# Five row minima and maxima of a closing check, moved one turn earlier on VectorE in a fused linear-attention and mixture-of-experts kernel

## The chip, the cores and the metric

The kernel runs on one core of one Trainium2 chip. The metric is the device time in microseconds (us) of one execution. The time of a kernel is the median of its runs.

## The reference, cut to what matters

A gated linear attention over 4 batches, 8 heads, 768 tokens and a head width of 48 gives `x` of 3072 tokens by 384. A mixture of 8 experts follows, whose gate is balanced in eight rounds:

```python
for t in range(S):
    state = f[:, :, t, :, None] * state + np.einsum('bhd,bhe->bhde', k[:, :, t], v[:, :, t])
    y[:, :, t] = np.einsum('bhd,bhde->bhe', q[:, :, t], state)
...
P = np.exp(logits - logits.max())          # logits = x @ w_gate
for _ in range(8):
    P /= P.sum(1, keepdims=True) + 1e-09
    P /= P.sum(0, keepdims=True) + 1e-09
    P *= N / E
for e in range(E):
    h = np.maximum(x @ w1[e], 0.0)
    out += P[:, e:e + 1] * (h @ w2[e])
```

All operands are float32. The kernel computes each product from pairs of float16 numbers (a high and a low part, names ending in `h` and `l`), which is good only while the inputs lie in certain bounds. So it also computes a flag, and where the flag is set, a slower general version (`general`) runs behind the fast one.

## The kernel before, in words

`fast` does the attention and, between its steps, part of experts 0 and 1. After some 520 us it goes over to the long last stage, which the change concerns: experts 2 to 7 in 48 **periods** (`period`, one for each expert, half of the hidden width and batch, in the order of `ORDER`). A period has 15 **slots**. In each slot TensorE gets, in this order:

- 6 products of layer 1 (`kb_A` to `kb_F`, six PSUM banks of the pool `pk`; a scheme with 15 products in place of 18, so that VectorE and ScalarE have to add and copy banks between: `EVENTS`, L1188 to L1198);
- whatever the slot's **jobs** issue (`plan`);
- 4 or 5 products of layer 2 of the period before (`layer2`).

Layer 2 works in **groups** of 12 products that add up in one PSUM tile `kyps`, 6 groups a period. The tile is then read once, either by ScalarE (`yt`, L1094, with GpSimd adding it to the output at L1095) or by VectorE (`acc`, L1091). These tiles come from the pool `psm` with the tag "m", which has **two** buffers.

The order on each engine is the order of the program text: `mm` puts every product behind the one before on TensorE, and `pin` does the same for each instruction on VectorE, ScalarE and GpSimd. So the place in the text at which an instruction is issued is its place in the engine's queue. Which of the two buffers a tile gets, and whom it must wait for, is settled by the framework when the kernel is built: a tile can take a buffer once the last reader of the tile that was in it is done.

The jobs of a slot are short steps of generators. One of them is `all_checks`: it gets a **turn** in certain slots of the periods from the third on, namely slots 5, 10 and 13, slots 3 and 11, slot 5, and slots 3 and 11, over and over in four periods. A turn is one `next(checks, None)`, the last job of its slot. The turns go first to maxima of the weights, then to `guard`, and at the end to `verdict`. Its last part puts five columns of one number per partition (`g`, `[128, 7]`) through `partition_reduce` (L94): a transposition on TensorE makes a column a row of 128 numbers on one partition, in a tile `gd0_t` to `gd4_t` (`gd_t` in the profile), which comes from the pool `psm` with the tag "m" too; VectorE takes the row's minimum or maximum (L99, `gd_r`). A `yield` lies between the two, so the reduction is issued one turn after its transposition. After each reduction comes another `yield` (L812), so that a row takes two turns: ten turns for the five rows. Eight small operations on single numbers follow in two more turns (L813 to L821), the last of which writes the flag.

Two pieces of code name what is touched: the pool of two buffers, and the read of the tile.

```python
psm = ctx.enter_context(tc.tile_pool(name="psm", bufs=2, space=PSUM))
...
ps = psm.tile([128, DM], F32, name=f"kyps_{n}_{t}_{v}", tag="m")
...
ps = psp.tile([128, 128], F32, name=name + "_t", tag=tag)      # psp is psm, tag is "m"
```

Of the kernel before, what the change touches and what calls it, by code (L numbers as in the profile page):

```python
# [85 lines left out]
def consts(nc, pool):  # L86
    identf = pool.tile([128, 128], F32, name="identf")
    make_identity(nc, identf)
    onesf = pool.tile([128, 128], F32, name="onesf")
    nc.vector.memset(onesf, 1.0)  # L90
    return identf, onesf


def partition_reduce(nc, pool, psp, tag, identf, col, op, name, mm, pin):  # L94
    ps = psp.tile([128, 128], F32, name=name + "_t", tag=tag)
    mm(transpose=True, out=ps[0:1, :], in_=col, identity=identf)
    row = pool.tile([1, 1], F32, name=name + "_r")
    yield
    pin(nc.vector.tensor_reduce(out=row, in_=ps[0:1, :], axis=AX.X, op=op))  # L99
    return row  # L100

# [149 lines left out]
def fast(ctx, tc, qkf, vbd, wg, w1, w2, out, flag):  # L251
    nc = tc.nc
# [17 lines left out]
    def pin(ins):  # L270
        engine = ins.ins.engine
        if fixed[0]:
            if engine in last:
                behind(ins, last[engine])
            last[engine] = ins
        return ins
# [7 lines left out]
    cst = ctx.enter_context(tc.tile_pool(name="cst", bufs=1))  # L284
# [8 lines left out]
    psm = ctx.enter_context(tc.tile_pool(name="psm", bufs=2, space=PSUM))  # L293
# [4 lines left out]
    identf, onesf = consts(nc, cst)  # L298
# [496 lines left out]
    def verdict():  # L795
        g = cst.tile([128, 7], F32, name="wg6")
        pin(nc.vector.tensor_reduce(out=g[:, 0:2], in_=wmx, axis=AX.X, op=ALU.min))
        pin(nc.vector.tensor_reduce(out=g[:, 2:4], in_=wmx, axis=AX.X, op=ALU.max))
        xm = xmx.rearrange("p b k -> p (b k)")
        pin(nc.vector.tensor_reduce(out=g[:, 4:5], in_=xm, axis=AX.X, op=ALU.max))  # L800
        pin(nc.vector.tensor_reduce(out=g[:, 6:7], in_=xm, axis=AX.X, op=ALU.min))
        yield
        pin(nc.vector.tensor_scalar(out=okm[:, 1:2], in0=g[:, 0:1], scalar1=W1_MIN / W1S, scalar2=None, op0=ALU.is_ge))
        pin(nc.vector.tensor_scalar(out=okm[:, 2:3], in0=g[:, 1:2], scalar1=W2_MIN / W2S, scalar2=None, op0=ALU.is_ge))
        pin(nc.vector.tensor_scalar(out=okm[:, 3:4], in0=g[:, 3:4], scalar1=W2_MAX / W2S, scalar2=None, op0=ALU.is_le))
        pin(nc.vector.tensor_reduce(out=g[:, 5:6], in_=okm, axis=AX.X, op=ALU.min))
        yield
        yield
        rows = []
        for n, (col, op) in enumerate(((5, ALU.min), (4, ALU.max), (2, ALU.max), (6, ALU.min), (0, ALU.min))):  # L810
            rows.append((yield from partition_reduce(nc, cst, psm, "m", identf, g[:, col:col + 1], op, f"gd{n}", mm, pin)))
            yield  # L812
        pin(nc.vector.tensor_tensor(out=rows[1], in0=rows[1], in1=rows[2], op=ALU.mult))  # L813
        pin(nc.vector.tensor_tensor(out=rows[3], in0=rows[3], in1=rows[4], op=ALU.mult))
        pin(nc.vector.tensor_scalar(out=rows[3], in0=rows[3], scalar1=BALANCE, scalar2=None, op0=ALU.mult))
        pin(nc.vector.tensor_tensor(out=rows[3], in0=rows[1], in1=rows[3], op=ALU.is_le))
        pin(nc.vector.tensor_scalar(out=rows[1], in0=rows[1], scalar1=XW1_MAX / W1S, scalar2=None, op0=ALU.is_le))
        yield
        pin(nc.vector.tensor_tensor(out=rows[0], in0=rows[0], in1=rows[1], op=ALU.mult))
        pin(nc.vector.tensor_tensor(out=rows[0], in0=rows[0], in1=rows[3], op=ALU.mult))  # L820
        pin(nc.vector.tensor_scalar(out=flag, in0=rows[0], scalar1=FLAG_AT, scalar2=None, op0=ALU.is_lt))  # L821
# [79 lines left out]
    live, g = list(early), -4  # L901
# [217 lines left out]
    def all_checks():  # L1119
        todo = [(e, j, k) for e in range(NE) for k in (1, 2) for j in range(4)]  # L1120
        raws_ = []
        for i in range(len(todo) + 1):
            if i < len(todo):
                e, j, k = todo[i]
                raw = lp.tile([128, 768], F32, name=f"wm_{k}_{e}_{j}", tag="wmax", bufs=2)
                nc.sync.dma_start(out=raw, in_=(w1 if k == 1 else w2)[e, j].rearrange("p a f -> p (a f)"))
                raws_.append(raw)
            if i:
                e, j, k = todo[i - 1]
                pin(nc.vector.tensor_reduce(out=wmx[:, k - 1, 4 * e + j:4 * e + j + 1], in_=raws_[i - 1], axis=AX.X, op=ALU.max, apply_absolute_value=True))  # L1130
            yield
        yield from guard()
        yield from verdict()
# [146 lines left out]
```

## Time and profile before

| | |
|---|---|
| Median of 3 runs | 1570.7 us (1570.29 to 1571.0) |
| Profiled execution, its own time | 1571.04 us |
| Its span, first to last instruction | 1569.3 us |
| Granted TensorE clock, mean | 0.99 |
| TensorE busy | 1524.3 us, 97% of the span |
| VectorE, ScalarE, GpSimd busy | 1085.6, 781.2 and 533.1 us |
| The five transpositions `gd_t` | 1394.1 to 1488.3 us |
| The five reductions `gd_r` | 1407.0 to 1500.9 us |
| The flag written | 1533.7 us |

The span starts with the first instruction of the program; 1.7 us of the profiled execution lie around it. In rows of the timeline the first number is the start, the second the length, both in us; a bracket at the end says how long the engine had been idle and who released it. Products overlap on TensorE: the length of one is longer than the step to the next, and the step is what it costs the engine. In the views of waits the three numbers are the total in us, how often, and the longest.

### The profile page before, as it was taken

The page shows a single profiled execution, that of the slowest core. Times are in us where ns is not written, and L with a number is a line of the kernel's source. Part 1 is how long each engine was busy: PE and PEld are TensorE (multiplying, and loading weights), DVE is VectorE, ACT ScalarE, POOL GpSimd, SP SyncE. Part 2 cuts the span into 40 slices and gives each one's busy share as a digit, 9 for nine tenths or more (in the row PEclk, how much of TensorE's full clock was granted, in tenths as well). Part 3 has the DMA queues.
Part 4 walks back from the last instruction along what each step waited for, and adds up shares of the span by engine and source line. Part 5 has one row for each costly group of instructions (what it writes and reads, how often), then busy time and mean ns, then how long its engine had stood idle before and what let it go on. Part 6 is the DMA issues. An engine that isn't in the chain of part 4 may idle for free.

```text
span 1569.3 us, 32417 instructions
## 1 busy us (share of the span) xinstructions
PE 1524.3 (97%) x13425; PEld 1107.7 (71%) x13425; DVE 1085.6 (69%) x1798; ACT 781.2 (50%) x1493; POOL 533.1 (34%) x668
## 2 busy tenths in 40 slices
PE   6799999999999999999999999999999999999998
PEld 4688886666555777777777777777777777776675
DVE  7687987884766766677767677666666666755554
ACT  6655555554343655555445554445444445444432
POOL 1644444354519012333333332223322223222211
PEclk9799999999999999999999999999999999999999
DMA  8355554541001222232322222121212111100011
GB/s 267 93 135 133 137 124 115 134 112 38 21 26 56 61 61 82 66 91 67 91 66 85 74 85 61 50 62 41 71 42 64 40 43 51 31 11 11 6 51 69
DMA packets 91502, 114.85 MB, mean 73 GB/s; under 512 B 52464, under 2 KB 68976, under 8 KB 91344
## 3 DMA queue, kind: packets, MB, share of 16 engines
q1 hardware_dynamic: 91344, 112.68, 25.5%
q8 instruction: 107, 1.75, 0.5%
q14 instruction: 51, 0.42, 0.1%
HBM read 88.41 MB, written 14.16 MB: 65 GB/s over the span
## 4 chain that ended last, share of the span: by engine, by line
PE 67%; DVE 1%; ACT 1%; issue 0%; POOL 0%; ACTq 0%; DVEq 0%; POOLq 0%
PE kyps L279 35%; PE kb_B L279 8%; PE kb_A L279 8%; PE kb_D L279 6%; PE kb_C L279 4%; PE kb_E L279 2%; PE kb_F L279 2%; PE yps L279 1%; PE hps L279 1%; ACT yt L1094 0%; DVE acc L1091 0%; ACT kh L1195 0%; ACT cp L1188 0%; DVE cp L1193 0%; DVE kb_F L1190 0%
## 5 line engine op out<-in xcount | busy, mean ns | idle before, releaser
L1095 POOL TENSOR_TENSOR acc<-acc,yt 128x384 f32<-128x384 f32 x172 | 173.4, 1008 | 637.7 <-ACT yt L1094 637.7
L279 PE MATMUL kyps<-k2h,kh 128*128 128x384 f16 x1152 | 375.5, 326 | 6.1 <-ACT yt L1094 2.5
L279 PE MATMUL kyps<-k2l,kh 128*128 128x384 f16 x1152 | 375.5, 326 | 0.0
L279 PE MATMUL kyps<-k2h,kl 128*128 128x384 f16 x1152 | 375.5, 326 | 0.0
L279 PEld LDWEIGHTS <-k1h 128*128 128x128 f16 x2880 | 281.5, 98 | 70.4
L279 PEld LDWEIGHTS <-kh 128*128 128x128 f16 x2304 | 225.4, 98 | 103.9
L1094 ACT ACTIVATE yt<-kyps,pes 128x384 f32<-128x384 f32 x172 | 99.8, 580 | 326.4 <-PE kyps L279 324.5
L279 PEld LDWEIGHTS <-k1l 128*128 128x128 f16 x1440 | 140.7, 98 | 63.4 <-issue 6.2
L1091 DVE SCALAR_TENSOR_TENSOR acc<-kyps,pes,acc 128x384 f32<-128x384 f32 x92 | 56.8, 618 | 176.0 <-PE kyps L279 176.0
L279 PEld LDWEIGHTS <-kl 128*128 128x128 f16 x1152 | 112.7, 98 | 53.3 <-issue 9.3
L1188 ACT ACTIVATE cp<-kb_A 128x512 f32<-128x512 f32 x144 | 86.0, 597 | 86.6 <-PE kb_A L279 86.1
L279 PE MATMUL yps<-w2h,hl 128*128 128x384 f16 x384 | 126.4, 329 | 1.5 <-DVE hl L441 0.8
L279 PE MATMUL yps<-w2l,hh 128*128 128x384 f16 x384 | 126.0, 328 | 0.8 <-DVE w2l L362 0.8
L279 PE MATMUL yps<-w2h,hh 128*128 128x384 f16 x384 | 126.3, 329 | 0.3 <-DVE hl L394 0.3
L279 PEld LDWEIGHTS <-w1h 128*128 128x128 f16 x1344 | 99.0, 99 | 38.5 <-ACT w1h L341 5.9
L1188 ACT ACTIVATE cp<-kb_B 128x512 f32<-128x512 f32 x144 | 86.9, 604 | 52.0 <-DVE kb_B L1190 50.5
L1193 DVE TENSOR_TENSOR cp<-kb_D,cp 128x512 f32<-128x512 f32 x144 | 98.8, 686 | 16.2 <-PE kb_D L279 15.2
L279 PEld LDWEIGHTS <-hh 128*128 128x128 f16 x768 | 75.4, 99 | 47.8 <-issue 3.1
L279 PE MATMUL hps<-xh,w1h 128*128 128x128 f16 (+1 forms) x672 | 86.1, 260 | 5.6 <-ACT w1h L341 5.5
L279 PE MATMUL hps<-xl,w1h 128*128 128x128 f16 (+1 forms) x672 | 85.3, 260 | 0.4 <-DVE xl L616 0.2
L279 PE MATMUL hps<-xh,w1l 128*128 128x128 f16 (+1 forms) x672 | 84.3, 259 | 0.6 <-DVE w1l L362 0.6
L279 PE MATMUL kb_A<-xbh,k1h 128*128 128x256 f16 x288 | 78.5, 273 | 0.8 <-ACT yr L411 0.6
(249 smaller groups left out, 3645.0 us busy)
## 6 DMA issues: line engine op xcount, KB each, us to landing
wm<-in_w_dram SPq DMA_DIRECT2D x64, 384.0 KB, 3.0
q<-in_qkf_dram SPq DMA_DIRECT2D x23, 672.0 KB, 5.0
vr<-in_vbd_dram SPq DMA_DIRECT2D x24, 384.0 KB, 3.5
ys<-yr SPq DMA_DIRECT2D x48, 192.0 KB, 2.5
k1r<-in_w_dram SPq DMA_DIRECT2D x24, 384.0 KB, 3.1
k2r<-in_w_dram SPq DMA_DIRECT2D x24, 384.0 KB, 3.0
yb<-ys SPq DMA_DIRECT2D x48, 192.0 KB, 2.4
out_dram<-acc SPq DMA_DIRECT2D x24, 192.0 KB, 1.9
```

Of the source, the lines that this page charges most:

```text
L279: ins = (nc.tensor.transpose if transpose else nc.tensor.matmul)(**kw)
L1091: pin(nc.vector.scalar_tensor_tensor(out=y, in0=ps, scalar=p, in1=y, op0=ALU.mult, op1=ALU.add))
L1094: pin(nc.scalar.activation(out=yt, in_=ps, func=AF.Copy, scale=p))
L1095: pin(nc.gpsimd.tensor_tensor(out=y, in0=y, in1=yt, op=ALU.add))
L1188: pin(nc.scalar.activation(out=fresh(ev[2]), in_=bk, func=AF.Copy))
L1193: pin(nc.vector.tensor_tensor(out=fresh(ev[4]), in0=bk, in1=old, op=ALU.add if ev[2] == '+' else ALU.subtract))
```

## The change

The reduction is issued directly behind its transposition, in the same turn. The turn that held it stays, as an empty one behind: the rows still take two turns each, and what follows them has the turn that it had. The instructions are the same and as many as before.

```diff
     ps = psp.tile([128, 128], F32, name=name + "_t", tag=tag)
     mm(transpose=True, out=ps[0:1, :], in_=col, identity=identf)
     row = pool.tile([1, 1], F32, name=name + "_r")
-    yield
     pin(nc.vector.tensor_reduce(out=row, in_=ps[0:1, :], axis=AX.X, op=op))
     return row
...
         for n, (col, op) in enumerate(((5, ALU.min), (4, ALU.max), (2, ALU.max), (6, ALU.min), (0, ALU.min))):
-            rows.append((yield from partition_reduce(nc, cst, psm, "m", identf, g[:, col:col + 1], op, f"gd{n}", mm, pin)))
+            rows.append(partition_reduce(nc, cst, psm, "m", identf, g[:, col:col + 1], op, f"gd{n}", mm, pin))
+            yield
             yield
```

## The prediction

> **What bounds the kernel now.** I read the page first, then the waits of TensorE, then the tile of the changed step, and last the timeline around it.
>
> ```profile
> span 1569.3 us, 32417 instructions
> PE 1524.3 (97%) x13425; PEld 1107.7 (71%) x13425; DVE 1085.6 (69%) x1798; ACT 781.2 (50%) x1493; POOL 533.1 (34%) x668
> PE 67%; DVE 1%; ACT 1%; issue 0%; POOL 0%; ACTq 0%; DVEq 0%; POOLq 0%
> ```
>
> TensorE is busy for 97% of the span and holds nearly all that is named in the chain that ended last. In the last stage a microsecond is gained only where TensorE stands, and then it is gained in full as long as nothing else comes late.
>
> ```profile
> PE kyps L279 <- ACT yt L1094: 2.5, 4, 0.7
> PE kyps L279 <- DVE acc L1091: 2.1, 3, 0.7
> PE kyps L279 <- DVE gd_r L99: 1.0, 2, 0.5
> PE kb_A L279 <- ACT cp L1188: 1.6, 4, 0.8
> ```
>
> These are TensorE's waits over the whole span, as far as they belong to the last stage (beside two on `cp` for `kb_D`). The first three lines make 9 waits and 5.6 us, all of them of the first product of a layer 2 group (`kyps`) for somebody who reads a PSUM tile. Where are they? One row of the groups of instructions, asked for 1387.75 to 1504.87 us alone, holds all nine:
>
> ```profile
> L279 PE MATMUL kyps<-k2h,kh 128*128 128x384 f16 x121 | 39.4, 325 | 6.1 <-ACT yt L1094 2.5 <-DVE acc L1091 2.1 <-DVE gd_r L99 1.0
> L279 PE MATMUL gd_t<-identf,wg x5: 272/273/273, 1394.1 to 1488.3; 128*1 128x128 f32 x5
> L99 DVE TENSOR_REDUCE gd_r<-gd_t x5: 267/267/269, 1407.0 to 1500.9; 1x1 f32<-1x128 f32 x5
> ```
>
> So in a stage of 48 periods the groups wait only in those five in which the rows `gd_t` are made and read. From these rows, too, the first row lies in its buffer from 1394.1 until the end of its reduction, 1407.0 + 0.27 = 1407.3: 13 us, more than half a period. In that time one of the two buffers of `psm` is taken, and the groups have to share the other. The timeline shows what that does:
>
> ```profile
> 1392.54 0.27 PE L279 MATMUL kb_A<-xal,k1h 128*128 128x256 f16 x1
> 1394.12 0.27 PE L279 MATMUL gd_t<-identf,wg 128*1 128x128 f32 x1
> 1394.23 0.33 PE L279 MATMUL kyps<-k2l,kh 128*128 128x384 f16 x1
> 1397.05 0.27 PE L279 MATMUL kb_A<-xbl,k1h 128*128 128x256 f16 x1
> 1397.38 0.32 PE L279 MATMUL kyps<-k2h,kh 128*128 128x384 f16 x1
> 1400.47 0.33 PE L279 MATMUL kyps<-k2l,kh 128*128 128x384 f16 x1
> 1401.51 0.32 PE L279 MATMUL kyps<-k2h,kh 128*128 128x384 f16 x1 [0.71 <-DVE acc L1091]
> ```
> ```profile
> 1392.92 0.70 DVE L1190 TENSOR_TENSOR kb_A<-kb_A,cp 128x512 f32<-128x512 f32 x1 [0.63 <-PE kb_A L279]
> 1396.71 0.62 DVE L1091 SCALAR_TENSOR_TENSOR acc<-kyps,pes,acc 128x384 f32<-128x384 f32 x1 [3.09 <-PE kyps L279]
> 1400.84 0.62 DVE L1091 SCALAR_TENSOR_TENSOR acc<-kyps,pes,acc 128x384 f32<-128x384 f32 x1 [1.19 <-PE kyps L279]
> ```
>
> The last product of a group starts at 1400.47; VectorE reads the group from 1400.84 to 1401.46; the next group's first product starts at 1401.51, a step of 1.04 us where two such products normally lie 0.16 apart. It waited for the one free buffer: 0.88 us, of which the bracket names 0.71. Where six layer 1 products lie between two groups (1397.05 to 1397.38) most of the read is covered, and 0.33 - 0.11 = 0.22 us are left, without a bracket. So the nine named waits are not all. I size the loss by the periods instead, by the first `kb_F` product of each, which stands in the same slot every time:
>
> ```profile
> 1344.56 0.27 PE L279 MATMUL kb_F<-xah,k1h 128*128 128x256 f16 x1
> 1366.16 0.27 PE L279 MATMUL kb_F<-xah,k1h 128*128 128x256 f16 x1
> 1387.75 0.27 PE L279 MATMUL kb_F<-xah,k1h 128*128 128x256 f16 x1
> 1504.87 0.27 PE L279 MATMUL kb_F<-xah,k1h 128*128 128x256 f16 x1
> 1526.88 0.27 PE L279 MATMUL kb_F<-xah,k1h 128*128 128x256 f16 x1
> ```
>
> The two periods before the rows take 21.60 and 21.59 us. The five with the rows take 1504.87 - 1387.75 = 117.12 us. Five undisturbed ones would take 5 x 21.595 = 107.98, so 9.14 us are extra. Five transpositions are in that, at a step of 0.11 us each (1394.12 to 1394.23): 0.55 us, which stay. **8.6 us** are waits.
>
> **The change, part by part.**
>
> *What goes.* The row's hold shrinks. The transposition takes 0.27 us, the hand-over from TensorE to VectorE 0.11 (the last `kb_A` product above ends at 1392.54 + 0.27 = 1392.81, VectorE starts on it at 1392.92), the reduction 0.27: some 0.65 us in place of 13. The row that starts at 1394.12 is read by 1394.8; the next group starts at 1397.4. It then finds a free buffer, as groups do in every other period, and the same holds for the groups behind it. What remains are the groups that start directly behind a row:
>
> ```profile
> 1420.28 0.27 PE L279 MATMUL gd_t<-identf,wg 128*1 128x128 f32 x1
> 1420.50 0.32 PE L279 MATMUL kyps<-k2h,kh 128*128 128x384 f16 x1
> 1475.99 0.27 PE L279 MATMUL gd_t<-identf,wg 128*1 128x128 f32 x1
> 1476.23 0.32 PE L279 MATMUL kyps<-k2h,kh 128*128 128x384 f16 x1
> ```
>
> The second and the fourth row are such: the steps are 0.22 and 0.24 us instead of 0.11. There the new group takes the buffer of the group that ended just now, whose reader is not quite done; the row has the other one. No earlier reduction can spare that, since it comes after the transposition. These 0.11 + 0.13 = 0.24 us stay, and 8.6 - 0.24 = **8.4 us** go. The bounds of this term: 8.6 if these two steps vanish as well, and 8.6 - 2 x 0.88 = 6.8 if both groups are given the row's buffer instead and wait as long as the longest wait above.
>
> *What comes.* No instruction is added, and no DMA, nothing of ScalarE, GpSimd or SyncE is moved. Five reductions stand earlier in VectorE's queue and wait there for TensorE to reach the transposition. Everything behind them in that queue waits too: the next additions of banks, the reads of groups, the low parts `kl`; behind those stand ScalarE's copies, and behind these TensorE's next products on the bank. What has VectorE to do at the five places? Behind the first row it stands idle until 1396.71, 3.09 us by the bracket above. The others:
>
> ```profile
> 1422.07 0.70 DVE L1190 TENSOR_TENSOR kb_B<-kb_B,cp 128x512 f32<-128x512 f32 x1 [1.62 <-PE kb_B L279]
> 1453.50 0.69 DVE L1193 TENSOR_TENSOR cp<-kb_D,cp 128x512 f32<-128x512 f32 x1
> 1454.11 0.68 DVE L1198 SCALAR_TENSOR_TENSOR kl<-kb_B,kh 128x512 f16<-128x512 f32 x1
> 1455.22 0.70 DVE L1190 TENSOR_TENSOR kb_E<-kb_E,cp 128x512 f32<-128x512 f32 x1 [0.42 <-PE kb_E L279]
> 1476.70 0.70 DVE L1190 TENSOR_TENSOR kb_D<-kb_D,cp 128x512 f32<-128x512 f32 x1 [2.01 <-ACT cp L1188]
> 1490.87 0.62 DVE L1091 SCALAR_TENSOR_TENSOR acc<-kyps,pes,acc 128x384 f32<-128x384 f32 x1 [3.09 <-PE kyps L279]
> ```
> ```profile
> 1453.44 0.27 PE L279 MATMUL gd_t<-identf,wg 128*1 128x128 f32 x1
> 1456.72 0.27 PE L279 MATMUL kb_D<-xah,k1h 128*128 128x256 f16 x1
> ```
>
> Behind the second row (1420.28) VectorE's next work starts at 1422.07, after 1.62 us of idling: the reduction, due at 1420.66 and over at 1420.93, fits. Behind the fourth (1475.99) it is due at 1476.37 and over by 1476.64; the addition behind it waited for ScalarE until 1476.70. Behind the fifth (1488.28) nothing starts before 1490.87. Only the third row (1453.44) meets work: the reduction could start at 1453.82, and the read of `kb_D` that started at 1453.50 would wait until 1454.09, 0.6 us later. It would then end at 1454.78, and `kb_D` is next written at 1456.72; if that product came earlier by the longest wait above, 0.88 us, there would still be 1.06 us of slack. The delay is gone again at 1455.22, where VectorE idled 0.42 us. So I put the moved reductions at **0**. If that cover were gone, the third would cost its 0.6 us; below nothing the term can't go, as the same reductions stand in the queue a turn later today, where they take 0.27 us from nobody whom TensorE waits for except in the two `gd_r` waits, counted already.
>
> One rule speaks against the change. The Trainium skill ("PSUM — Partial Sum Buffer", section "Engine vs sequencer instructions") says that the queues of ScalarE, VectorE and GpSimd are strictly first in, first out: so a reduction that waits holds all behind it, however ready. By the rows, four of the five hold nothing. If instead every hold reached TensorE with its whole 0.65 us, the sum would be 8.4 - 5 x 0.65 = 5.1 us.
>
> *The sum.* The profiled execution took 1571.04 us, 1.74 more than its span, and less 8.4 makes that 1562.6. The median of the runs is 0.34 lower, 1570.7; with the same saving it becomes **1562.3 us**, 0.53% less. (About 0.2%, 3.1 us, is what a measurement of this kernel can tell from no change.) What is late next is nothing in these periods: they become like those ahead of them. The flag's last operations keep their turns.
>
> **The rivals.**
>
> *Each row still costs one wait.* The framework hands out the two buffers when the kernel is built, by its own estimate of who is done first. It may give the group behind every row the row's buffer, with a read that comes late because VectorE had something else in hand. Then one full wait of 0.88 us remains per row: 5 x 0.88 = 4.4 us, a saving of 4.2, and 1566.5 us. For it: two groups did take the buffer of a row (the two `gd_r` waits). Against it: in both the row's hold ended first, and three of five rows have over 2 us until the next group starts.
>
> *The wait moves into VectorE's queue and costs more there: slower.* The queue rule above is its ground. VectorE's additions read what the slot before has made, so at worst VectorE arrives at the reduction a whole slot ahead, 21.6 / 15 = 1.44 us, stands until the row is there, and all behind it is late by that and by the hold of 0.65: 2.09 us. If TensorE pays each in full, that is 5 x 2.09 = 10.4 against 8.6 saved: 1570.7 + 1.8 = 1572.5 us. It decides from 8.6 / 5 = 1.7 us a row. Against it: at four places VectorE idled anyway, for 1.62 to 3.09 us.
>
> *The change frees nothing, or it is given back.* The waits could have another cause than the rows' hold, or the buffers might be tied up until the turn's end as before; 1570.7 us. Against it: all nine waits lie in the five periods, and two are put down to `gd_r` itself. For giving back speaks only that `kb_A` waits for ScalarE's copies at times, 1.6 us in four waits over the span; a period of 22.01 us follows the rows (1504.87 to 1526.88), so 0.4 us per period can appear where TensorE is undisturbed.
>
> **How the numbers follow.** The forecast has 0.80, one wait per row 0.13, nothing gained 0.04, slower by the queue 0.03. The range of the likeliest case: without any remainder 1570.7 - 8.6 = 1562.1, less the half spread of the runs (0.35) and rounding, 1561.5; at the other end 1570.7 - 6.8 = 1563.9 with the row's buffer taken twice, 0.6 for the third row and 0.3 for the spread, 1564.8. The other cases, 2 in 10, are left out. The first two cases are faster by over 0.2% (1566.5 is 0.27% less): 0.93. Nothing gained is within, and so is the slower case at its worked price (0.11%), for which I count a third of its chance: 0.05. The rest of it, where the queue costs more than that price, is slower: 0.02.
>
> **What would show it.** Right: the first `kb_F` products of the five periods lie about 21.7 us apart (21.6 and a transposition); TensorE's waits of `kyps` for `yt`, `acc` and `gd_r` sum to under 1 us; each reduction starts 0.4 to 0.6 us behind its transposition. Half right: `kyps <- gd_r` has five waits of up to 0.9 us. Wrong: the waits for `yt` and `acc` stay as they are (another cause), or `kb_A` and `kb_D` wait for `cp` several us more than before (VectorE's queue).

## The result and the profile after

The changed kernel takes 1562.49 us (median of 5 runs, 1562.02 to 1563.09); the kernel before 1570.7 (5 runs). The ratio is 0.9948, with a 95% interval of 0.9934 to 0.9963: 8.2 us less. The forecast was 1562.3 and 8.4. The profiled execution took 1563.09 us.

The lines of the page, the groups of instructions on TensorE asked for the five periods with the rows, the tile of the row, and the first `kb_F` product of each of those periods and of the one behind them (in this file L278 is the old L279, L98 the old L99; in the files of the experiments the line numbers shift by a few, the names of the tiles stay):

```profile
span 1561.4 us, 32416 instructions
PE 1522.8 (98%) x13425; PEld 1108.4 (71%) x13425; DVE 1086.1 (70%) x1798; ACT 781.4 (50%) x1493; POOL 533.0 (34%) x668
```
```profile
L278 PE MATMUL kyps<-k2h,kh 128*128 128x384 f16 x121 | 39.4, 326 | 0.0
L278 PE MATMUL gd_t<-identf,wg x5: 272/272/273, 1394.2 to 1481.5; 128*1 128x128 f32 x5
L98 DVE TENSOR_REDUCE gd_r<-gd_t x5: 278/279/280, 1394.5 to 1481.8; 1x1 f32<-1x128 f32 x5
...
1387.85 0.27 PE L278 MATMUL kb_F<-xah,k1h 128*128 128x256 f16 x1
1409.84 0.27 PE L278 MATMUL kb_F<-xah,k1h 128*128 128x256 f16 x1
1431.64 0.27 PE L278 MATMUL kb_F<-xah,k1h 128*128 128x256 f16 x1
1453.35 0.27 PE L278 MATMUL kb_F<-xah,k1h 128*128 128x256 f16 x1
1475.11 0.27 PE L278 MATMUL kb_F<-xah,k1h 128*128 128x256 f16 x1
1496.82 0.27 PE L278 MATMUL kb_F<-xah,k1h 128*128 128x256 f16 x1
```

TensorE's products are the same and as many, and its busy time is the same but for 1.5 us. What went is idling: the first products of the groups, which had waited 6.1 us, wait 0.0. The five periods take 1496.82 - 1387.85 = 108.97 us instead of 117.12, so 8.15 of the 8.2 us were lost there. Each reduction starts 0.3 us behind its transposition, where it was 4 to 20 us. At the first row:

```profile
1397.15 0.27 PE L278 MATMUL kb_A<-xbl,k1h 128*128 128x256 f16 x1
1397.26 0.33 PE L278 MATMUL kyps<-k2h,kh 128*128 128x384 f16 x1
...
1400.36 0.33 PE L278 MATMUL kyps<-k2l,kh 128*128 128x384 f16 x1
1400.52 0.33 PE L278 MATMUL kyps<-k2h,kh 128*128 128x384 f16 x1
```
```profile
1394.52 0.28 DVE L98 TENSOR_REDUCE gd_r<-gd_t 1x1 f32<-1x128 f32 x1 [0.81 <-PE gd_t L278]
1396.81 0.62 DVE L1091 SCALAR_TENSOR_TENSOR acc<-kyps,pes,acc 128x384 f32<-128x384 f32 x1 [2.00 <-PE kyps L278]
```

The group behind the row starts in step, 0.11 us after the product ahead of it, where it was 0.33; the group after that one starts 0.16 us after the last product of its forerunner, where it was 1.04. VectorE stood 0.81 us at the head of its queue for the transposition, had the row read at 1394.80, and then idled 2.00 us more. Its wait cost nobody.

### The profile page after: what moved, and what is told of

It reads as the page before. It is cut to its first block, busy times and chain, and to the rows that moved or that the text cites. A ratio compares the mean times of both kernels' runs of the same rounds, so it can differ in the third digit from the quotient of the medians.

```text
span 1561.4 us, 32416 instructions
## 1 busy us (share of the span) xinstructions
PE 1522.8 (98%) x13425; PEld 1108.4 (71%) x13425; DVE 1086.1 (70%) x1798; ACT 781.4 (50%) x1493; POOL 533.0 (34%) x668
## 4 chain that ended last, share of the span: by engine, by line
PE 67%; DVE 1%; ACT 1%; issue 0%; POOL 0%; DVEq 0%; ACTq 0%; POOLq 0%
PE kyps L278 35%; PE kb_A L278 8%; PE kb_B L278 8%; PE kb_D L278 6%; PE kb_C L278 4%; PE kb_E L278 2%; PE kb_F L278 2%; PE yps L278 1%; PE hps L278 1%; ACT kh L1195 0%; ACT cp L1188 0%; DVE cp L1193 0%; DVE kb_F L1190 0%; DVE acc L1091 0%; ACT yt L1094 0%
## 5 line engine op out<-in xcount | busy, mean ns | idle before, releaser
L278 PE MATMUL kyps<-k2l,kh 128*128 128x384 f16 x1152 | 375.5, 326 | 0.0
L278 PE MATMUL kyps<-k2h,kl 128*128 128x384 f16 x1152 | 375.5, 326 | 0.0
L278 PE MATMUL kyps<-k2h,kh 128*128 128x384 f16 x1152 | 375.5, 326 | 0.0
L278 PEld LDWEIGHTS <-k1h 128*128 128x128 f16 x2880 | 281.5, 98 | 70.4
L278 PEld LDWEIGHTS <-kh 128*128 128x128 f16 x2304 | 225.4, 98 | 103.9
L278 PEld LDWEIGHTS <-k1l 128*128 128x128 f16 x1440 | 140.6, 98 | 64.1 <-issue 6.6
L278 PEld LDWEIGHTS <-kl 128*128 128x128 f16 x1152 | 112.7, 98 | 44.7
L278 PE MATMUL yps<-w2h,hl 128*128 128x384 f16 x384 | 126.1, 328 | 1.5 <-DVE hl L440 0.8
L278 PE MATMUL yps<-w2l,hh 128*128 128x384 f16 x384 | 125.9, 328 | 0.8 <-DVE w2l L361 0.8
L278 PE MATMUL yps<-w2h,hh 128*128 128x384 f16 x384 | 126.3, 329 | 0.3 <-DVE hl L393 0.3
L278 PEld LDWEIGHTS <-w1h 128*128 128x128 f16 x1344 | 99.3, 100 | 37.6 <-ACT w1h L340 5.0
L278 PEld LDWEIGHTS <-hh 128*128 128x128 f16 x768 | 75.3, 99 | 47.7 <-issue 3.0
L278 PE MATMUL hps<-xh,w1h 128*128 128x128 f16 (+1 forms) x672 | 86.5, 260 | 4.7 <-ACT w1h L340 4.5
L278 PE MATMUL hps<-xl,w1h 128*128 128x128 f16 (+1 forms) x672 | 85.3, 261 | 0.4 <-DVE xl L615 0.2
L278 PE MATMUL hps<-xh,w1l 128*128 128x128 f16 (+1 forms) x672 | 84.9, 261 | 0.6 <-DVE w1l L361 0.6
L278 PE MATMUL kb_A<-xbh,k1h 128*128 128x256 f16 x288 | 78.5, 273 | 0.8 <-ACT yr L410 0.6
```

Source lines behind the costliest of these rows:

```text
L278: ins = (nc.tensor.transpose if transpose else nc.tensor.matmul)(**kw)
```

## The experiments

Two theories were to be told apart. **H**: the row's tile holds one of the two buffers of `psm`, and the groups wait for the other. **Q**: what counts is where the reductions stand in VectorE's queue. Times are compared with runs of the kernel before on the same chip.

**The row read at once, and held all the same** (`read_twice`). The reduction is made early, and again a turn later:

```diff
     pin(nc.vector.tensor_reduce(out=row, in_=ps[0:1, :], axis=AX.X, op=op))
+    yield
+    again = pool.tile([1, 1], F32, name=name + "_s")
+    pin(nc.vector.tensor_reduce(out=again, in_=ps[0:1, :], axis=AX.X, op=op))
     return row
```

> Each row is reduced at once, as in the changed kernel, and the same reduction is made a second time one turn later, so that the tile is held as long as before. H: the waits come back, 1570.7 us, with 66 us of hold in all and TensorE's waits of the groups at 5 to 6 us. Q: the reduction that counts is early, so 1562.5 us and at most 1 us for five more reductions of 0.27.

Measured: 1570.62 us, ratio 1.0002 (0.9993 to 1.0012). TensorE's waits for groups, by the view of its waits:

```profile
PE kyps L281 <- ACT yt L1096: 2.5, 4, 0.7
PE kyps L281 <- DVE acc L1093: 2.1, 3, 0.7
PE kyps L281 <- DVE gd_s L101: 1.0, 2, 0.5
```

They are those of the kernel before to the tenth, with the second reduction `gd_s` in the place of `gd_r`. The early reductions, waiting in VectorE's queue as in the changed kernel, neither help nor harm: reading early saves nothing while the tile is held. One form of Q is left, since `gd_s` stands where `gd_r` stood: that a reduction at that late place in VectorE's queue is what costs. The next kernels have such late reductions and no tile.

**No tile at all, reductions in their old place** (`rows_by_dma`, `rows_by_one_dma`, `six_writes`). The columns go to a DRAM tile and come back as rows into SBUF. In the first of these kernels, made from the kernel before, each row has a write and a read of its own into one SBUF row:

```diff
-            rows.append((yield from partition_reduce(nc, cst, psm, "m", identf, g[:, col:col + 1], op, f"gd{n}", mm, pin)))
+            drow = dp.tile([128, 1], F32, name=f"gd{n}_d")
+            nc.sync.dma_start(out=drow, in_=g[:, col:col + 1])
+            nc.sync.dma_start(out=identf[0:1, :], in_=drow.rearrange("p o -> o p"))
+            row = cst.tile([1, 1], F32, name=f"gd{n}_r")
+            yield
+            pin(nc.vector.tensor_reduce(out=row, in_=identf[0:1, :], axis=AX.X, op=op))
```

> Theory H (the row's tile holds one of the two PSUM buffers, and the layer 2 groups wait for the other): with the rows brought over by DMA and no PSUM tile and no transposition for them, the reductions standing one turn later as in the kernel before, all the extra of the five periods goes, 8.6 us of waits and 0.55 of transpositions: 1570.7 - 9.15 = 1561.5 us. Theory Q (what counts is the place of the reductions in VectorE's queue, or VectorE's work in the later turns): the place is that of the kernel before, so about 1570.7 less the transpositions, 1570.1 us.

Measured: 1567.71 us, ratio 0.9983 (0.9973 to 0.9992), between the two. First the row of the groups on TensorE, asked for 1387 to 1500 us; then the end of a stop around 1390 us that this kernel brought with it, on VectorE, ScalarE and TensorE:

```profile
L279 PE MATMUL kyps<-k2h,kh 128*128 128x384 f16 x120 | 39.5, 329 | 0.0
...
1393.01 0.70 DVE L1196 TENSOR_TENSOR kb_F<-kb_F,cp 128x512 f32<-128x512 f32 x1 [5.58 <-remote]
1393.14 0.58 ACT L1100 ACTIVATE yt<-kyps,pes 128x384 f32<-128x384 f32 x1 [5.08 <-remote]
1395.48 0.37 PE L279 MATMUL kb_A<-xah,k1h 128*128 128x256 f16 x1 [3.73 <-ACT cp L1194]
```

No group waits, as H says. But VectorE and ScalarE both stop for over 5 us, until 1393, and TensorE with them for 3.7. The five writes are issued from 1376.9 to 1381.3 us and land 9.0 to 19.7 us later; their packets all start before 1383, and none of any queue starts from there to 1396, so the stop falls into the time between packets and landing. So I took the rows over in one write and two reads that don't share a buffer:

```diff
+        drow = dp.tile([128, 7], F32, name="gd_d")
+        nc.sync.dma_start(out=drow, in_=g)
         yield
+        cells = lp.tile([128, 768], F32, name="gd_c", tag="wmax", bufs=2)[0:1, :]
+        nc.sync.dma_start(out=cells[:, 0:640].rearrange("o (p c) -> o p c", c=5), in_=drow[:, 2:7].rearrange("p (o c) -> o p c", o=1))
+        nc.sync.dma_start(out=cells[:, 640:768], in_=drow[:, 0:1].rearrange("p o -> o p"))
         yield
```

> The rows by DMA again, no PSUM tile, no transposition, reductions one turn later as in the kernel before; but with one write of seven columns (128 packets) in place of five of one column (640), and two reads a turn later, so that the rows do not wait for each other. In the first such kernel no group waited, but VectorE and ScalarE stood from 1387 to 1393 us while the 4-byte packets were under way, and TensorE lost 3.7 us in one wait and some 1.7 us at a lower clock behind it. H: without that, 1567.7 - 5.4 = 1562.3 us or a little less, by the sum 1570.7 - 9.15 + 0.28 (a wait at kb_C that shows where groups don't wait) = 1561.8 us. If the loss belonged to late reductions instead of the packets: 1567.7 again.

Measured: 1562.15 us, ratio 0.9944 (0.9928 to 0.9961).

```profile
1387.75 0.27 PE L279 MATMUL kb_F<-xah,k1h 128*128 128x256 f16 x1
1496.00 0.27 PE L279 MATMUL kb_F<-xah,k1h 128*128 128x256 f16 x1
```

The five periods take 108.25 us, 0.27 more than undisturbed ones: with no tile and no transposition the extra is gone, though every reduction stands a turn late, and the 0.27 is a wait of another kind (next section). So late reductions cost nothing by themselves: H holds, and Q falls in its last form too. The stop of the first such kernel went as well. Was it the number of 4-byte packets?

> The kernel with the rows by one write and two reads, but with the one write split into six of one column each (768 packets of 4 bytes, where the kernel with a write per row had 640). If the stop of VectorE and ScalarE and the 3.7 us wait of kb_A in that kernel came from the many 4-byte packets, they show again here: 1562.2 + 5 = 1567 us. If they came from the rows waiting for each other on the DMA queue (the reads into one buffer), there is no such stop: 1562.2 us.

Measured in a single run: 1561.32 us beside 1570.17 for the kernel before, and no stop, with 768 packets of 4 bytes written. So it wasn't their number; what stopped the two engines stays open (last section).

**One row held** (`second_row_held`). The `yield` stands ahead of the reduction for the second row only (`if name == "gd1": yield`, and one `yield` less behind it).

> Only the second row is read a turn later, as in the kernel before; the other four as in the changed one. H: the groups behind that row wait again. In the kernel before, five groups started inside its hold, with steps that were 0.87, 0.23, 0.83, 0.24 and 0.72 us too long, 2.9 us: 1562.5 + 2.9 = 1565.4 us. A rival, that each row costs the same whatever its hold: a fifth of 8.2, 1.6 us, 1564.1 us.

Measured: 1565.07 us, ratio 0.9965 (0.9952 to 0.9977).

```profile
PE kyps L280 <- DVE acc L1094: 0.7, 1, 0.7
PE kyps L280 <- ACT yt L1097: 0.7, 1, 0.7
PE kyps L280 <- DVE gd_r L100: 0.6, 1, 0.6
```
```profile
1387.16 0.27 PE L280 MATMUL kb_F<-xah,k1h 128*128 128x256 f16 x1
1498.93 0.27 PE L280 MATMUL kb_F<-xah,k1h 128*128 128x256 f16 x1
```

The five periods take 111.77 us, 2.80 more than in the changed kernel; 2.9 was forecast from the steps of the five groups that start inside this row's hold, and an equal share for each row would be 1.6. The longest hold (20.6 us of 66) costs a third of the whole.

**Held twice as long** (`held_two_turns`). Both `yield`s of a row stand ahead of its reduction.

> Each reduction stands two turns behind its transposition, in the turn of the next row. H: a buffer is taken without a break from 1394 to about 1520 us, 120 us in place of 66; in the kernel before 66 us of hold cost 8.6 us, so 15.6 us, 7 more than before: 1577.7 us, and more if the next transposition has to wait for the reduction of the row before. A fixed cost per row, or Q: no change, 1570.7 us.

Measured: 1578.08 us, ratio 1.005 (1.0033 to 1.0066): 7.7 us slower than the kernel before, where 7.0 was worked out.

```profile
PE kyps L280 <- ACT yt L1094: 6.9, 10, 0.7
PE kyps L280 <- DVE acc L1091: 3.5, 5, 0.7
PE kyps L280 <- DVE gd_r L100: 0.6, 1, 0.6
```

The longest of these waits is 0.7 us, as before; there are 16 in place of 9. The price goes by the groups that start while a row is held.

**VectorE made late** (`vector_late_1`, `vector_late_3`). Behind each reduction of the changed kernel stand one or three further ones, whose results nobody reads:

```diff
+            for i in range(3):
+                pin(nc.vector.tensor_reduce(out=junk, in_=lg.rearrange("p a e -> p (a e)")[:, None, :].to_broadcast([128, 4, NT * NE]), axis=AX.X, op=ALU.max))
             yield
```

> The changed kernel, with one idle reduction over 128 x 768 numbers (0.9 to 1.0 us, as the reduction over 128 x 768 at line 776 takes) behind each of the five on VectorE: everything behind them is late by that much more. The forecast's view (V: VectorE has idle time there): four of the five places have 1.1 us or more of idle time behind the reduction, the third has 1.06 us of slack towards kb_D: 1562.5 to 1563.0 us. The queue rival (each us on VectorE reaches TensorE): 5 x 0.95 = 4.75 us, 1567.2 us.

Measured: 1562.64 us, ratio 0.9947 (0.993 to 0.9963), 0.15 us from the changed kernel. With 5 x 0.93 us more behind the rows, the five periods take 108.96 us, to 0.01 us what they took without:

```profile
1387.80 0.27 PE L278 MATMUL kb_F<-xah,k1h 128*128 128x256 f16 x1
1496.76 0.27 PE L278 MATMUL kb_F<-xah,k1h 128*128 128x256 f16 x1
```

Idle time covered it at three places only. At the fourth row VectorE idles 0.12 us behind the reduction, not 1.1, and the addition to `kb_D` behind it came 0.7 us late; as at the third row, TensorE's next need of the bank lay far enough off.

> The same with three such reductions, 2.85 us behind each row. V: the idle time behind the rows (1.1 to 2.3 us) and the slack towards TensorE's next need (1 to 2 us) together cover most; what goes beyond is up to 1 us a row: 1562.5 to 1567 us, with the waits at kb_A, kb_C and kb_D for copies. The queue rival: 5 x 2.85 = 14.3 us, 1576.8 us.

Measured: 1565.19 us, ratio 0.9963 (0.9951 to 0.9976), 2.7 us over the changed kernel for 14.3 us of work. It all comes from two places, the third row and the fourth:

```profile
1450.01 2.90 DVE L813 TENSOR_REDUCE junk<-lg 128x4 f32<-128x768 f32 x3
1452.83 0.68 DVE L1196 TENSOR_TENSOR cp<-kb_D,cp 128x512 f32<-128x512 f32 x1
```
```profile
1453.57 0.27 PE L278 MATMUL kb_D<-xah,k1h 128*128 128x256 f16 x1 [1.52 <-DVE cp L1196]
1476.32 0.27 PE L278 MATMUL kb_D<-xah,k1h 128*128 128x256 f16 x1 [0.83 <-DVE cp L1196]
```

At the third row VectorE's read of `kb_D` came 2.8 us late (1452.83 us, 1450.01 in the changed kernel), and TensorE's next product on that bank waited 1.52; at the fourth it waited 0.83. At the other three places 2.9 us cost TensorE nothing: part of it fell into idle time, and the rest (0.8 us at the first row, where the read of the group starts at 1397.56 in place of 1396.81) was over before TensorE needed the result.

**One instruction more on ScalarE** (`scalar_shift`), for a small wait that the forecast had not got (next section): in `verdict`, ahead of the rows,

```diff
+        pin(nc.scalar.activation(out=cst.tile([128, 1], F32, name="junk"), in_=xm[:, 0:1], func=AF.Copy))
```

> The changed kernel with one copy of 128 numbers added on ScalarE ahead of the first row. The changed kernel shows one wait that is new: kb_C for a copy of ScalarE, 0.28 us too long a step in the first row's period, behind a read of a group that starts 0.28 us late; that read starts late by as much in the kernel before, where the groups' own waits covered it. If the delay belongs to a place in ScalarE's instruction stream, it moves to a neighbouring instruction and the wait at kb_C changes or goes; if it belongs to the data or the moment, it stays. Time 1562.5 us, within 0.3.

Measured in a single run: 1561.86 us. The period of the first row, which took 1409.84 - 1387.85 = 21.99 us in the changed kernel:

```profile
1387.37 0.27 PE L278 MATMUL kb_F<-xah,k1h 128*128 128x256 f16 x1
1409.08 0.27 PE L278 MATMUL kb_F<-xah,k1h 128*128 128x256 f16 x1
```

It takes 21.71 us: the wait is gone with one instruction's shift of ScalarE's stream.

## Why the prediction was right, step by step

**The bound.** Right. The time saved lies in the five periods, 8.15 of 8.2 us, and nothing came late behind them. The periods of 22.01 us and over that follow the rows, with their waits of `kb_A`, are as they were.

**The cause.** Right, and now shown from both sides: with the row read early and its tile held all the same, the whole time is back (`read_twice`); with the reductions late and no tile held, it goes (`rows_by_one_dma`).

**The size of what goes, 8.6 us by the periods.** Right. Had I added up the nine waits that bear a name, 5.6 us, I should have been a third short; the steps that are 0.2 us too long and bear no name, and the part of each step that its bracket leaves out, make the rest.

**The two groups directly behind a row, 0.24 us.** The mechanism is right, the size 0.08 us too large. At the second and the fourth row of the changed kernel:

```profile
1419.13 0.27 PE L278 MATMUL gd_t<-identf,wg 128*1 128x128 f32 x1
1419.35 0.32 PE L278 MATMUL kyps<-k2h,kh 128*128 128x384 f16 x1
1469.82 0.27 PE L278 MATMUL gd_t<-identf,wg 128*1 128x128 f32 x1
1470.06 0.32 PE L278 MATMUL kyps<-k2h,kh 128*128 128x384 f16 x1
```

The steps are 0.22 and 0.24 us, as they were, and the readers of the groups that ended just before are done 0.05 us ahead of the new ones: VectorE at 1418.68 + 0.62 = 1419.30, ScalarE at 1469.43 + 0.58 = 1470.01. But the fourth row's period is not longer by the whole of its step. Elsewhere the step into the first `kb_C` product is 0.24 us where a period has no other wait; here it is 0.16 (1470.55 to 1470.71), and the period takes 21.76 us, 0.05 more than 21.6 and a transposition. So the two groups cost 0.16 us, not 0.24. The rival by which each row still costs a wait of its own (1566.5 us) falls: `kyps` waits for no `gd_r` at all.

**VectorE's queue, 0.** Right, with the third row as the only one that meets work:

```profile
1448.82 0.70 DVE L1190 TENSOR_TENSOR kb_D<-kb_D,cp 128x512 f32<-128x512 f32 x1 [0.74 <-ACT cp L1188]
1449.80 0.28 DVE L98 TENSOR_REDUCE gd_r<-gd_t 1x1 f32<-1x128 f32 x1 [0.28 <-PE gd_t L278]
1450.01 0.67 DVE L1193 TENSOR_TENSOR cp<-kb_D,cp 128x512 f32<-128x512 f32 x1
```

The read of `kb_D` starts directly behind the reduction, for which VectorE had stood 0.28 us. The rule of the Trainium skill ("PSUM — Partial Sum Buffer", section "Engine vs sequencer instructions") that this queue is strictly first in, first out is borne out here: the read did not overtake. What it costs depends on what is behind: 5 x 0.93 us more cost nothing, 5 x 2.9 us cost 2.7. The slower rival, by which every microsecond reaches TensorE, falls with that: it had its break-even at 1.7 us a row, and with 2.9 us a row more TensorE paid 2.7 us for all five rows together. One sign was a little off: each reduction starts 0.31 us behind its transposition, not 0.4 to 0.6, since the hand-over that was read off `kb_A` (0.11 us) is 0.04 here.

**What was missed: 0.28 us.** The five periods are 108.97 - 107.98 = 0.99 us longer than undisturbed ones; 0.55 + 0.24 = 0.79 were forecast. In place of that stand 0.55 for the transpositions, 0.16 for the two groups and 0.28 in the first row's period (21.99 us), for a wait that had not been in the list:

```profile
1403.62 0.33 PE L278 MATMUL kyps<-k2l,kh 128*128 128x384 f16 x1
1404.92 0.33 PE L278 MATMUL kyps<-k2h,kh 128*128 128x384 f16 x1
1405.44 0.27 PE L278 MATMUL kb_C<-xah,k1h 128*128 128x256 f16 x1 [0.19 <-ACT cp L1188]
```
```profile
1404.32 0.58 ACT L1094 ACTIVATE yt<-kyps,pes 128x384 f32<-128x384 f32 x1 [3.49 <-PE kyps L278]
1404.80 0.59 ACT L1188 ACTIVATE cp<-kb_C 128x512 f32<-128x512 f32 x1
```

The group's last product ends at 1403.62 + 0.33 = 1403.95, and ScalarE, idle, starts to read it 0.37 us later, where 0.09 is usual; its copy of `kb_C` behind that is late, and TensorE needs the bank. In the kernel before, the same read was 0.37 us late too (1404.60 + 0.33 = 1404.93 to 1405.30), but the next group had to wait for it anyway: the loss sat inside the larger one. It shows in `rows_by_one_dma` as well, in `rows_by_dma` at the same instruction although that comes 5 us later there, and goes when an instruction is added ahead on ScalarE. So it belongs to a place in ScalarE's instruction stream; what happens at that place the traces don't show. The forecast's sentence that nothing is late next was wrong by this much, 0.28 of 8.4 us. That the whole came within 0.2 us is luck in part, as the 0.08 us too much for the two groups stands against it.

## What to carry to other kernels

A small tile in a ring of two buffers is dear by the time from its first write to its last read, not by its size: one row of 128 numbers, left unread for a turn, made the main loop single-buffered and cost 0.2 to 0.9 us for every group that started meanwhile. Put its read directly behind its write, even if the reading engine must wait at the head of its queue, and look in the profile at whether that engine has idle time there. Size such a loss by the length of a repeating unit with and without it: here waits of 0.2 us carried no name in the profile, and a wait of 0.88 us was named with 0.71.

## What the runs showed of the hardware

In `rows_by_dma`, after TensorE had stood for 3.9 us, its clock fell. The columns are the stretch, its length, busy time of TensorE, its weight loads, VectorE, ScalarE and GpSimd (with counts), the granted clock, the DMA share and GB/s:

```profile
1380.00:1391.60 11.60, 11.60 (x88) 8.45 (x87) 4.64 (x11) 4.48 (x9) 2.00 (x2) 1.00 0.01 0
1391.60:1395.48 3.88, 0.15 (x1) 0.00 (x0) 2.47 (x5) 2.31 (x5) 0.99 (x1) 0.99 0.00 0
1395.48:1398.90 3.42, 3.42 (x15) 2.01 (x15) 1.91 (x4) 1.36 (x3) 0.27 (x1) 0.51 0.05 5
```

For 3.42 us the granted clock is 0.51, and steps are 0.21 us instead of 0.11: 1.7 us lost on top of the wait. The Trainium skill ("TensorE: Matmul & The Clock Gate", "Part 1: The HAM clock gate") gives about 3.4 us of idling as what brings the clock to half, and as much work to bring it back; this trace agrees, with 3.9 us of standing and 3.42 us at 0.51. The waits of up to 0.9 us in the kernel before left the clock at full: 1.00 in each of the five periods.

In the same kernel the five writes of 128 single numbers, which lie side by side in DRAM, took 9.0 to 19.7 us to land (median 14.3). In `six_writes`, with the numbers 28 bytes apart, the median was 2.2 us. VectorE and ScalarE stood during the first and not during the second. Whether the spacing made the landing slow, and whether the slow landing stopped the engines, was not tried: the two kernels also differ in their reads.
